# Loads that wait for the third-last store instead of the second-last, in a decode-step gradient kernel

## The chip, the cores and the metric

The kernel runs on one core of a Trainium2 chip. The metric is device time in microseconds (us) of one execution; lower is better. Executions of one kernel agree within about 0.3%.

## The reference, cut to what matters

One decode step of attention over a cache plus a gated MLP, in parallel, and the gradients of all inputs:

```python
xn  = layernorm(x)                                     # x: (1, 1, 640)
q   = xn @ wq                                          # 32 heads of 128
p   = softmax(q @ k_cache^T * 128**-0.5)               # k_cache, v_cache: (1, 32, 8192, 128), bf16
out = x + (p @ v_cache) @ wo + (silu(xn @ w1) * (xn @ w3)) @ w2
# returned: out, and its gradients for x, k_cache, v_cache, wq, wo, w1, w3, w2
```

The caches are 64 tiles of 2 MB (32 heads, K and V). Each is read once, and the gradient for it, a dense tile of the same size, is written once. Together with the weights, their gradients and the instruction fetch, 304.63 MB pass through the DMA engines.

## The kernel before: the parts that matter

A K or V tile fills one of ten SBUF slots. VectorE writes the gradient over the tile in place, the slot is stored, and a later tile is loaded into it. All cache loads and stores go through one function, `fifo`, which issues on the SyncE queue in program order. An issue that has to wait for a semaphore holds up all issues behind it.

```python
def fifo(out_, in_):
    nc.sync.dma_start(out_, in_)

free_slots = [...]                      # ten tiles, 128 x 8192 bf16
pending = [K of head 0, V of head 0, K of head 1, ...]
lag = [1]

def load_next():
    if not pending or len(free_slots) < lag[0]:
        return
    kind, h = pending.pop(0)
    t = free_slots.pop(0)               # the slot that was freed first
    fifo(t[:], (kc if kind == "K" else vc)[h])
    kv_tiles[(kind, h)] = t
...                                     # six loads; four slots lent to the MLP's weights
lag[0] = 2

def store(kind, h):
    t = kv_tiles.pop((kind, h))
    ...
    fifo((dkc if kind == "K" else dvc)[h], t[:])
    free_slots.append(t)
    load_next()
```

With `lag` 2, the load after a store takes not the slot just stored but the one stored before it, and so waits for the landing of the second-last store.

Between heads 1 and 2 the kernel does the MLP. It overwrites the weights in the four lent slots with their gradients, stores these through another queue (POOL's), and gives the slots back, one load each:

```python
nc.gpsimd.dma_start(out_8[...], w2a);  ...;  free_slots.append(mD);  load_next()
for wi in range(2):
    ...
    nc.gpsimd.dma_start(dv[:, 0:NA, :], wa)
    free_slots.append((mA, mB)[wi])
    load_next()
    ...
free_slots.append(mC)
load_next()
```

Of the kernel before, what the change touches and what calls it, by code (L numbers as in the profile page):

```python
# [21 lines left out]
def kernel(  # L22
# [93 lines left out]
    lag = [1]  # L116
# [35 lines left out]
    for _ in range(2):  # L152
        load_next()

    lag[0] = 2

    ident_f = consts.tile([P, P], F32, name="ident_f")
    make_identity(nc, ident_f[:])
# [595 lines left out]
```

## Time and profile before

| | before |
|---|---|
| time, median of the first 3 runs | 751.14 us (750.63 to 751.73) |
| span of the profile | 749.7 us |
| PE / VectorE busy | 79% / 60% |
| DMA, the main data queue alone | 89.1% of 16 engines' span |
| 2 MB store, issue to landing | 22.2 us |
| 2 MB load, issue to landing | 16.6 us (K), 16.7 us (V) |

First the page of before: its busy line (engine, us, share, instructions), its queue table (packets, MB, share of 16 engines' span) and its issue table (count, KB each, median us to landing).

```profile
PE 593.0 (79%) x11263; PEld 565.3 (75%) x11263; DVE 447.7 (60%) x739; ACT 333.3 (44%) x668; POOL 30.4 (4%) x45
...
q1 hardware_dynamic: 22736, 276.39, 89.1%
q0 software_dynamic: 5984, 26.30, 8.7%
q8 instruction: 88, 1.44, 0.7%
...
out_dram<-kv SPq DMA_DIRECT2D x64, 2048.0 KB, 22.2
kv<-in_A_k_cache_dram SPq DMA_DIRECT2D x32, 2048.0 KB, 16.6
```

The three queues add up to 98.5% of all that 16 DMA engines have. No compute engine comes near that.

Where is DMA not full? This is the view by stretches of before. The last two numbers of a line are the DMA share and GB/s.

```profile
120.00:140.00 20.00, 18.25 (x372) 17.54 (x372) 11.65 (x16) 10.59 (x21) 0.00 (x0) 1.00 0.84 319
300.00:660.00 360.00, 298.14 (x5622) 286.91 (x5618) 212.96 (x325) 169.16 (x338) 11.43 (x14) 0.92 1.01 414
730.00:746.00 16.00, 0.00 (x0) 0.00 (x0) 0.00 (x0) 0.00 (x0) 0.00 (x0) 0.50 0.68 286
```

There is one hole, at 120-140 us. The timeline of the SyncE queue in before (start, us taken to issue, what) shows what the queue did there:

```profile
116.70 0.33 SPq L101 DMA_DIRECT2D kv<-in_A_v_cache_dram  x1
130.49 0.33 SPq L101 DMA_DIRECT2D kv<-in_A_k_cache_dram  x1
130.87 1.19 SPq L101 DMA_DIRECT2D out_dram<-kv  x1
```

Between 116.70 and 130.49 us nothing is issued. The load at 130.49 (K of head 6) goes into a slot that held the MLP's w3; its gradient's store on POOL's queue was issued at 90.25 and landed at 130.4. Right behind that load stands the store of head 2's V. VectorE had finished that tile by 111.8 us, as its timeline in before shows (the two halves of V's gradient, then the first half of K's):

```profile
107.36 4.48 DVE L379 TENSOR_TENSOR kv<-qd,P 128x4096 bf16<-128x4096 bf16 x2
111.76 2.28 DVE L379 TENSOR_TENSOR kv<-qd,U 128x4096 bf16<-128x4096 bf16 x1
```

The last thing to read is who among the DMA engines is late. A 2 MB transfer raises its semaphore 16 times as its parts land, and the trace has the time of every increment. One load of before in the steady state (issued 509.89), in us, sorted:

```
before: 517.8 517.9 518.0 518.0 518.1 518.1 518.7 519.8 519.9 520.3 520.5 520.7 520.8 522.6 523.3 526.8
```

Fifteen increments come within 5.5 us and the last one 3.5 us after the fifteenth. One part of every transfer is late; I call whatever carries it the lagging engine. A transfer counts as landed only at the sixteenth increment. Over the transfers issued at 300-660 us, first and last increment lie 8.5 us apart on average (the skew).

### The profile page before, as it was taken

The numbers are of one execution on the slowest core, as the hardware profiler recorded it, in microseconds if no ns is written. First come the engines' busy times: TensorE is split into PE (matmuls) and PEld (weight loads), VectorE is DVE, ScalarE is ACT, GpSimd is POOL, SyncE is SP. The second block draws the span as 40 slices with busy tenths as digits, with TensorE's granted clock in tenths as the row PEclk, the third lists the DMA queues.
The fourth block names the chain that finished last, engine by engine and source line by source line (L and its number), as shares of the span: only waits on it lengthen the run. The fifth ranks groups of instructions, "written<-read, shape, count | busy, mean of one in ns | idle before, by whom it ended". The sixth has DMA issues, their size and how long they took to land.

```text
span 749.7 us, 25013 instructions
## 1 busy us (share of the span) xinstructions
PE 593.0 (79%) x11263; PEld 565.3 (75%) x11263; DVE 447.7 (60%) x739; ACT 333.3 (44%) x668; POOL 30.4 (4%) x45
## 2 busy tenths in 40 slices
PE   1987798999999868798786978879688898878810
PEld 1885598988998868698686868878688887868800
DVE  4269837677667645657464664657367475646670
ACT  1641065555565435445354544435355354535400
POOL 0100200000000100000000000000000000000000
PEclk9997799999999999999898998989899799999955
DMA  8999998999999999999999999999999999999995
GB/s 329 389 413 420 418 418 353 378 425 426 416 424 430 424 421 413 423 410 420 417 392 416 415 425 397 424 412 420 422 392 414 418 421 404 413 408 415 426 428 224
DMA packets 29136, 304.63 MB, mean 406 GB/s; under 512 B 2836, under 2 KB 5972, under 8 KB 12644
## 3 DMA queue, kind: packets, MB, share of 16 engines
q1 hardware_dynamic: 22736, 276.39, 89.1%
q0 software_dynamic: 5984, 26.30, 8.7%
q8 instruction: 88, 1.44, 0.7%
q10 hardware_dynamic: 308, 0.33, 0.2%
q14 instruction: 20, 0.16, 0.1%
HBM read 151.67 MB, written 151.34 MB: 404 GB/s over the span
## 4 chain that ended last, share of the span: by engine, by line
DMA 59%; PE 27%; DVE 8%; issue 2%; ACT 1%; SPq 1%; ACTq 0%; DVEq 0%
DMA out_dram<-kv 39%; DMA kv<-in_A_k_cache_dram 15%; PE pT L274 11%; DMA kv<-in_A_v_cache_dram 4%; PE hb L358 4%; DVE kv L379 3%; PE dA L293 3%; PE sA L293 3%; PE hb L373 3%; DVE U L365 1%; PE dh_ps L462 1%; PE acc L536 1%; PE gu_ps L451 1%; PE sA L320 1%; DVE kv L539 0%
## 5 line engine op out<-in xcount | busy, mean ns | idle before, releaser
L274 PE MATMUL pT<-ident_f,kv 128*128 128x128 f32 x2048 | 335.2, 288 | 67.8 <-DMA kv<-in_A_k_cache_dram 60.1
L276 ACT COPY KT<-pT 128x512 f32<-128x512 f32 x512 | 299.3, 586 | 183.8 <-PE pT L274 151.1
L274 PEld LDWEIGHTS pT<-ident_f,kv 128*128 128x128 f32 x2048 | 223.5, 145 | 72.2 <-issue 68.7
L293 PEld LDWEIGHTS <-KT 128*128 128x128 bf16 x4096 | 196.0, 100 | 19.9 <-issue 12.8
L379 DVE TENSOR_TENSOR kv<-qd,U 128x4096 bf16<-128x4096 bf16 x64 | 146.0, 2284 | 0.0
L379 DVE TENSOR_TENSOR kv<-qd,P 128x4096 bf16<-128x4096 bf16 x64 | 143.4, 2282 | 0.0
L293 PE MATMUL dA<-cz,KT 128*128 128x64 bf16 x2048 | 106.6, 196 | 8.8 <-ACT qd L310 6.6
L293 PE MATMUL sA<-cz,KT 128*128 128x64 bf16 x2048 | 103.0, 192 | 1.4 <-issue 1.4
L358 PEld LDWEIGHTS <-kv 128*128 128x128 bf16 x2048 | 80.8, 105 | 16.5 <-issue 16.5
L358 PE MATMUL hb<-P,kv 128*128 128x64 bf16 x2048 | 81.6, 201 | 14.3 <-DVE U L365 14.3
L375 ACT COPY od_g<-hb 128x2 f32<-128x2 f32 x32 | 5.1, 160 | 159.1 <-PE hb L373 159.1
L373 PE MATMUL hb<-U,kv 128*128 128x64 bf16 x2048 | 70.4, 194 | 5.0 <-issue 4.9
L373 PEld LDWEIGHTS <-kv 128*128 128x128 bf16 x2048 | 66.7, 98 | 5.7 <-issue 5.7
L349 DVE SCALAR_TENSOR_TENSOR U<-dA,P 128x64 bf16<-128x64 f32 x32 | 7.4, 233 | 90.2 <-PE dA L293 90.2
L316 DVE TENSOR_REDUCE mrow<-sA 128x1 f32<-128x64 f32 x32 | 7.2, 224 | 83.4 <-PE sA L293 83.4
L365 DVE SCALAR_TENSOR_TENSOR U<-dA,hb,P 128x128 bf16<-128x128 f32 x32 | 11.4, 355 | 35.3 <-PE hb L363 35.3
L429 DVE SCALAR_TENSOR_TENSOR wq_g<-wq_g,side 128x512 bf16<-128x512 bf16 x40 | 27.3, 682 | 0.0
L340 DVE RECIPROCAL rZ<-sA 128x1 f32<-128x1 f32 x32 | 5.4, 168 | 35.9 <-PE sA L334 35.0
L233 DVE SCALAR_TENSOR_TENSOR side<-wo_g,g_bc 128x640 bf16<-128x640 bf16 x32 | 26.2, 817 | 0.3
L323 DVE TENSOR_REDUCE negM<-sA 128x1 f32<-128x128 f32 x32 | 9.3, 291 | 18.6 <-PE sA L320 18.6
L424 POOL DMA_DIRECT2D out_dram<-wo_g x8 | 6.1, 761 | 291.1 <-DVE cz L298 255.7
L433 POOL DMA_DIRECT2D out_dram<-wq_g x8 | 6.9, 863 | 256.9 <-DVE wq_g L431 256.9
(134 smaller groups left out, 310.2 us busy)
## 6 DMA issues: line engine op xcount, KB each, us to landing
out_dram<-kv SPq DMA_DIRECT2D x64, 2048.0 KB, 22.2
kv<-in_A_k_cache_dram SPq DMA_DIRECT2D x32, 2048.0 KB, 16.6
kv<-in_A_v_cache_dram SPq DMA_DIRECT2D x32, 2048.0 KB, 16.7
out_dram<-wo_g POOLq DMA_DIRECT2D x8, 640.0 KB, 12.6
out_dram<-wq_g POOLq DMA_DIRECT2D x8, 640.0 KB, 13.5
wq_g<-in_A_wq_dram POOLq DMA_DIRECT2D x7, 640.0 KB, 13.9
wo_g<-in_A_wo_dram POOLq DMA_DIRECT2D x7, 640.0 KB, 19.6
kv<-in_B_w_dram SPq DMA_DIRECT2D x2, 1728.0 KB, 16.5
```

Source lines behind the costliest of these rows:

```text
L233: nc.vector.scalar_tensor_tensor(junk[:], G_["wo"][:, hh, :], 1.0, g_bc[:], ALU.mult, ALU.mult, accum_out=G_["do"][:, hh:hh + 1])
L274: nc.tensor.transpose(pT[:, k * P:(k + 1) * P], W3[:, 4 * c + k, :], ident_f[:])
L276: nc.scalar.copy(KT[:].rearrange("p k w -> p (k w)"), pT[:])
L293: nc.tensor.matmul(S_[kind][:, 0:J], lhsT=KTb[:, k, par, :], rhs=S_["cz"][:, o:o + J], start=(i == 0 and par == 0), stop=(par == 1), skip_ ...
L320: nc.tensor.matmul(S_["K"][:, J:J + P], lhsT=S_["mrow"][:].to_broadcast([P, P]), rhs=ident_f[:], start=False, stop=True, skip_group_check= ...
L323: nc.vector.tensor_reduce(S_["negM"][:], S_["K"][:, J:J + P], AX.X, ALU.max, negate=True)
L358: nc.tensor.matmul(S_["hb"][:, 0:RW], lhsT=V3[:, j, :], rhs=S_["P2"][:, j, 0:1].to_broadcast([P, RW]), start=(j == 0), stop=(j == J - 1), ...
L365: nc.vector.scalar_tensor_tensor(S_["U2"][:], S_["V"][:, 0:J].unsqueeze(2).to_broadcast([P, J, 2]), S_["hb"][:, 2 * RW:2 * RW + 1], S_["P2 ...
L373: nc.tensor.matmul(S_["hb"][:, RW:2 * RW], lhsT=K3[:, j, :], rhs=S_["U2"][:, j, 0:1].to_broadcast([P, RW]), start=False, stop=(j == J - 1) ...
L379: nc.vector.tensor_tensor(dst[:, lo * DH:hi * DH].rearrange("p (j a b) -> p j a b", a=DH // 2, b=2), vec.rearrange("p (a b) -> p a b", b=2 ...
L429: nc.vector.scalar_tensor_tensor(wq_g[:, ci, :], wq_g[:, ci, :], 1.0, dqb, ALU.mult, ALU.mult, accum_out=dxa[:, ci, g:g + 1])
L451: nc.tensor.matmul(gu_ps[0:rows, wi, b:b + 1], lhsT=wrow(wi, ci)[:, b * P:b * P + rows], rhs=xn_col_bf[:, ci:ci + 1], start=(ci == 0), sto ...
```

## The change

The intent is to let SyncE issue stores earlier and wait less. The diff is one number:

```diff
-    lag[0] = 2
+    lag[0] = 3
```

Load k still reuses the k-th freed slot, and still needs that slot's store to have landed. What changes is the order in the queue: from the third store on, each store goes ahead of one load. Around the hole (a number is a head):

```
before: ... load V5, load K6, store V2, load V6, store K2, load K7 ...
after:  ... load V5, store V2, load K6, store K2, load V6, store V3, load K7 ...
```

## The prediction

> **What bounds the kernel.** The DMA engines, not compute. The page of before: 304.63 MB in a span of 749.7 us; its queue table sums to over 98% of 16 engines' span, against PE 79% and DVE 60%. In 10 us windows the DMA share is about 1.0 except at 0-10 us (0.74), 120-140 us (0.81 and 0.87, at 340 and 298 GB/s instead of about 420) and the last 10 us. PE's waits for K loads (60.1 us, 21 waits) follow from the full queue: a load lands 16.6 us after its issue.
>
> The semaphore landings in the trace (16 increments per transfer) say more. First and last increment of a 2 MB transfer lie 8 to 10 us apart in the steady state: some engines lag. The leading engines complete transfers 4.9 us apart, then pause for the next issue; the last increments are 4.9 to 6.4 us apart without a pause. The laggard's work sets the time; SyncE's wait on stores (581.6 us) is back-pressure. The Trainium skill's "DMA: Bandwidth & Descriptors", section "Why a DMA increments its semaphore by 16 and not by 1", says that the engines of a transfer finish independently; this trace agrees.
>
> **What the change does.** It adds and removes no transfer. Load k reuses the k-th freed slot and needs that store's landing in both kernels. In the queue's order each store from the third on moves ahead of one load: load k stands behind store k+2 instead of k+1. At a load's issue about 5 transfers are in flight instead of 3. Loads come about one transfer (5 us) later in the stream. In the steady state about 4 finished tiles wait to be stored (near 433 us head 16's V is stored while PE is in head 19), so the stores that go first are ready and DMA stays full either way. I expect no gain there: the laggard's bytes are the same.
>
> **Where it can gain.** SyncE sits from 117 to 130.5 us on a load whose slot is freed by a POOL-queue weight-gradient store (issued 90.25, landed 130.4), while the store of V2, computed by about 112 us, is stuck behind it (issued 130.87). The queue drains: over 120-140 us 10 x (80 + 122) us GB/s is missing, about 4.8 us of transfer, 3.2 us of it idle. In the new order V2's store goes first, near 117 us: 5 us of work. I count 2 to 4 us, all on the critical path since DMA is full from there on; the total drops by about 2.5 us.
>
> **Where it can lose.** Deeper queues let the leading engines run further ahead (skew 12-18 us); if their traffic slows the laggard (stores 5.3-5.6 us ungated in the tail, 5.2-5.35 gated), 1 to 3 us come back. The last load lands about 5 us later, but in before it landed at 699.6, the last store was issued at 717.3 and the laggard was busy to 748.6: over 20 us of slack.
>
> **Prediction.** 748.6 us, 80% range 745 to 752. Over 2% faster 0.02, within 2% 0.96, over 2% slower 0.02.
>
> **What would show it.** V2's store issued near 117 us; no dip at 120-140 us; store latency up from 22.2 to near 32 us, load latency from 16.6 to 22-26; landing skew above 10 us; PE waits for loads up, not down; busy times and bytes unchanged.
>
> **What would make it wrong.** That the finished-tile backlog is too short, so that loads are held for stores still being computed and DMA gaps appear every head (slower by 1% or more); or that read/write order or depth itself changes the rate of the DMA engines.

## The result, and the profile after

| | before | after |
|---|---|---|
| time, median | 751.24 us (4 runs) | 747.95 us (4 runs, 747.36 to 749.01) |
| span of the profile | 749.7 us | 745.6 us |
| 2 MB store / K load, issue to landing | 22.2 / 16.6 us | 31.8 / 26.9 us |
| mean skew, issued at 300-660 us | 8.5 us | 17.9 us |

The ratio is 0.9958 with a 95% interval of 0.9941 to 0.9975: a real gain of about 0.4%, within 2%. The output is correct.

The page after, same rows as before:

```profile
PE 596.1 (80%) x11263; PEld 568.4 (76%) x11263; DVE 447.8 (60%) x739; ACT 333.4 (45%) x668; POOL 30.4 (4%) x45
...
q1 hardware_dynamic: 22736, 276.39, 88.5%
q0 software_dynamic: 5984, 26.30, 8.8%
q8 instruction: 88, 1.44, 0.7%
...
out_dram<-kv SPq DMA_DIRECT2D x64, 2048.0 KB, 31.8
kv<-in_A_k_cache_dram SPq DMA_DIRECT2D x32, 2048.0 KB, 26.9
```

The work is the same. Every transfer of a K or V tile takes about 10 us longer to land, because two more transfers stand in the queue before it.

The SyncE timeline after, in the same place:

```profile
116.55 0.33 SPq L101 DMA_DIRECT2D kv<-in_A_v_cache_dram  x1
116.93 0.81 SPq L101 DMA_DIRECT2D out_dram<-kv  x1
130.25 0.33 SPq L101 DMA_DIRECT2D kv<-in_A_k_cache_dram  x1
```

The load of K6 goes out at the same time as before, but the store of V2 no longer waits for it: 116.93 instead of 130.87 us. At 145.65 us head 2's K store has also fully landed, where before head 2's V store had only just landed (145.53). The run is then exactly one 2 MB store ahead.

The stretches after:

```profile
120.00:140.00 20.00, 17.91 (x375) 17.14 (x373) 11.53 (x18) 10.86 (x23) 0.00 (x0) 1.00 1.00 402
300.00:660.00 360.00, 296.64 (x5631) 285.92 (x5629) 213.81 (x324) 168.54 (x337) 11.44 (x14) 0.94 1.01 422
730.00:746.00 16.00, 0.00 (x0) 0.00 (x0) 0.00 (x0) 0.00 (x0) 0.00 (x0) 0.50 0.06 27
```

The hole is filled in this execution. In the profiles of the three repeats below it is filled in part: 363, 381 and 382 GB/s at 120-140 us, against 319 in before. There is also a second difference, and it invites a wrong story. In the long middle the mean rate rose from 414 to 422 GB/s, as if the deeper queue made DMA faster. The third line shows where that goes: in the last 16 us the DMA share is 0.06, which is one engine of sixteen (1/16 = 0.0625) at work. The landing increments of the last store say the same:

```
before: 739.2 739.3 739.3 739.4 739.5 739.9 740.1 740.5 742.0 742.0 742.1 742.8 743.1 743.3 743.7 748.6
after:  724.8 724.9 724.9 725.0 725.0 725.0 726.3 726.3 727.5 727.6 727.7 728.1 728.4 728.9 729.5 744.5
```

After the change, fifteen parts are done by 729.5 us and one works alone until 744.5. The fifteen finished 14 us earlier than in before; the sixteenth, which sets the time, 4.1 us earlier.

### The profile page after: what moved, and what is told of

The parts are those of the page before. It is cut to its first block, busy times and chain, and to the rows that moved or that the text cites. A ratio compares the mean times of both kernels' runs of the same rounds, so it can differ in the third digit from the quotient of the medians.

```text
span 745.6 us, 25013 instructions
## 1 busy us (share of the span) xinstructions
PE 596.1 (80%) x11263; PEld 568.4 (76%) x11263; DVE 447.8 (60%) x739; ACT 333.4 (45%) x668; POOL 30.4 (4%) x45
## 3 DMA queue, kind: packets, MB, share of 16 engines
q8 instruction: 88, 1.44, 0.7%
## 4 chain that ended last, share of the span: by engine, by line
DMA 48%; PE 39%; DVE 8%; issue 2%; ACT 1%; SPq 0%; ACTq 0%; DVEq 0%
DMA kv<-in_A_k_cache_dram 31%; PE pT L274 17%; DMA out_dram<-kv 13%; PE hb L358 6%; PE hb L373 4%; PE sA L293 4%; DMA kv<-in_A_v_cache_dram 4%; PE dA L293 4%; DVE kv L379 3%; DVE U L365 1%; PE sA L320 1%; PE dh_ps L462 1%; PE hb L363 1%; PE acc L536 1%; PE gu_ps L451 1%
## 5 line engine op out<-in xcount | busy, mean ns | idle before, releaser
L274 PE MATMUL pT<-ident_f,kv 128*128 128x128 f32 x2048 | 337.1, 289 | 67.4 <-DMA kv<-in_A_k_cache_dram 62.4
## 6 DMA issues: line engine op xcount, KB each, us to landing
out_dram<-kv SPq DMA_DIRECT2D x64, 2048.0 KB, 31.8
kv<-in_A_k_cache_dram SPq DMA_DIRECT2D x32, 2048.0 KB, 26.9
kv<-in_A_v_cache_dram SPq DMA_DIRECT2D x32, 2048.0 KB, 26.9
```

Of the source, the lines that this page charges most:

```text
L274: nc.tensor.transpose(pT[:, k * P:(k + 1) * P], W3[:, 4 * c + k, :], ident_f[:])
```

## The experiments

Two theories for the gain. **Theory A**: the single early stall. The store of V2 stuck behind the load of K6 left the lagging engine without work; filling that hole is the whole gain. **Theory B**: depth. With five transfers in flight instead of three, DMA runs at 422 instead of 414 GB/s in the steady state.

A question behind both: **why is one engine late?** The theory is that it also carries the PE's instruction fetch (queue q8); the rival is that the fetch is spread over all engines and costs nothing. (The runs below were made to decide this and do not; the kept traces speak against the theory.)

Twelve runs in three batches, each batch with the changed kernel itself and with its own runs of before (medians 751.82, 751.83 and 751.66 us). All were correct except one that is wrong on purpose.

| run | median us | ratio to before | 95% interval |
|---|---|---|---|
| changed kernel, batch 1 / 2 / 3 | 747.84 / 748.71 / 749.03 | 0.9948 / 0.9959 / 0.9956 | 0.9937-0.9960 / 0.9946-0.9972 / 0.9943-0.9970 |
| one exchange only, batch 1 / 3 | 749.32 / 748.54 | 0.9968 / 0.9951 | 0.9955-0.9981 / 0.9937-0.9965 |
| deep later only, batch 1 | 751.80 | 0.9997 | 0.9984-1.0011 |
| deep early only, batch 3 | 748.15 | 0.9953 | 0.9938-0.9968 |
| fourth-last store, batch 1 | 748.37 | 0.9953 | 0.9941-0.9965 |
| more small PE pairs, batch 2 | 752.40 | 1.0010 | 0.9997-1.0024 |
| the same columns in wide pairs, batch 2 | 749.72 | 0.9974 | 0.9961-0.9987 |
| fewer PE pairs, batch 2 | 742.83 | 0.9881 | 0.9866-0.9896 |
| half the pairs, right result, batch 3 | 806.17 | 1.0717 | 1.0696-1.0737 |

The changed kernel as the yardstick of its batch:

> The changed kernel again, in the rounds of the next three: about 748 us, 0.996 of before.

> The changed kernel, in the rounds of the next three: about 748 us.

> The changed kernel, in the rounds of the next three: about 748 us, ratio 0.995 to 0.996.

It came out as expected three times, at 0.9948 to 0.9959.

### One exchange only

The kernel before, but the load due when `mC` comes back is put off until after the next store. The queue differs from before's in one place: store V2 goes ahead of load K6. All later loads wait for the second-last store.

```diff
+    owed = []
 ...
         free_slots.append(mC)
-        load_next()
+        owed.append(1)
 ...                                    # in store()
         free_slots.append(t)
         load_next()
+        if owed:
+            owed.pop()
+            load_next()
```

> The kernel before with one single exchange in the SyncE queue: the store of head 2's V goes ahead of the load of head 6's K; everything later waits for the second-last store as before. Theory (the gain is one early stall of the lagging DMA engine): the whole gain, 747 to 749 us, ratio 0.995 to 0.997; V2's store issued near 117 us, no dip at 120-140 us, while the landing skew stays at 8 to 11 us and the rate over 300-660 us stays at before's 413 GB/s. Rival (a deeper queue in the steady state, 424 instead of 413 GB/s, is the gain): 750.5 to 752 us, ratio 0.999 to 1.001.

Measured 749.32 us, 0.9968. V2's store went out at 119.55 us, the skew stayed at 8.4 us and the steady rate at 414 GB/s, as in before. In this view by stretches of the one-exchange kernel only the first line has changed against before:

```profile
120.00:140.00 20.00, 18.46 (x377) 17.75 (x375) 11.84 (x16) 10.84 (x22) 0.00 (x0) 1.00 0.98 397
300.00:660.00 360.00, 298.25 (x5602) 287.31 (x5599) 211.68 (x329) 171.38 (x344) 11.46 (x14) 0.93 1.01 414
```

So most of the gain needs no depth at all. But beside the changed kernel of its batch (0.9948) 0.2% seemed to be missing, with intervals that just overlap. It was run again:

> The single exchange again, beside the changed kernel: if all of the gain is the one stall, the two agree within 0.5 us; if the other early exchanges count too, it lies 1 to 2 us above (0.997 against 0.995), as in the first batch.

The second time it was 748.54 us (0.9951), beside 749.03 us (0.9956) for the changed kernel. The gap of the first batch did not repeat. Within what these runs resolve, the single exchange gives the whole gain.

### Deep later only

```diff
+        if kind == "V" and h == 4:
+            lag[0] = 3
         load_next()
```

> The kernel before up to the store of head 4's V, then the third-last store as in the changed kernel. Theory: no gain, 750 to 752 us, ratio 0.9985 to 1.001, although the rate over 300-660 us rises to about 424 GB/s and the skew to 18-20 us; the dip at 120-140 us is there as in before. Rival (deeper queue): the whole gain, 747 to 749 us, ratio 0.995 to 0.997.

Measured 751.80 us, 0.9997: nothing. Yet everything that theory B points to is there; this is the view by stretches of this run:

```profile
120.00:140.00 20.00, 18.64 (x379) 17.91 (x379) 12.03 (x16) 11.17 (x22) 0.00 (x0) 1.00 0.88 333
300.00:660.00 360.00, 295.93 (x5630) 285.26 (x5630) 213.02 (x326) 167.00 (x335) 12.19 (x15) 0.93 1.01 421
730.00:746.00 16.00, 0.93 (x3) 0.58 (x3) 2.57 (x15) 0.00 (x0) 0.86 (x1) 0.50 0.29 112
```

The rate is 421 GB/s and the skew 17.9 us, as in the changed kernel, the hole at 120-140 us is still there, and the time is before's. Theory B has fallen. A higher mean rate over sixteen engines says nothing about the one that ends last.

### Deep early only

The complement: third-last store until V of head 4 is stored, then one owed load and second-last from there on.

```diff
+        if kind == "V" and h == 4:
+            lag[0] = 2
+            load_next()
```

> The complement of the run that is deep only later: third-last store until the store of head 4's V, then one owed load, then second-last. Theory (only the early stage counts): as the changed kernel within 0.5 us, ratio 0.995 to 0.996, with skew 8 to 11 us. Rival (the rest of the gain comes from depth later on): as the single exchange, 0.997.

Measured 748.15 us, 0.9953, with a skew of 8.2 us. The gain is made in the early stage, and it is kept without depth.

### The fourth-last store

```diff
-    lag[0] = 3
+    lag[0] = 4
```

> The fourth-last store instead of the third-last. Theory: nothing more to gain, 747 to 749 us, ratio 0.995 to 0.997; skew up to about 20 to 30 us, store latency near 42 us; the lagging engine's own work unchanged. Rival (depth is worth 3 us a step): 744 to 745.5 us, ratio 0.991 to 0.9925. Third possibility (stores not ready, loads held): slower than the changed kernel, 750 us or more.

Measured 748.37 us, 0.9953: the same as the changed kernel. A store now takes 39.0 us to land and the mean skew is 22 us. One more step of depth buys nothing, and it costs nothing either. Stores that are not ready yet do hold the queue now: SyncE waits 183.1 us in total for tiles that VectorE is still writing, against 31.9 us in the changed kernel and 7.4 us in before. DMA stays full all the same, with a share of 1.01 at 300-660 us.

### Why one engine is late: more and fewer PE instructions

PE's 11263 weight loads and 11263 matmuls are 22526 instructions, and q8 moved 1.44 MB: 64 bytes each, in 88 packets of 16 KB. The Trainium skill says in "Runtime: NRT & Kernel Launch", section "Instruction fetch mechanics", that a sequencer refills its instruction memory in 16 KiB blocks of 256 instructions through a DMA queue of its own, and calls the cost mostly hidden. The size agrees with this trace. Whether the cost is hidden was tried on the changed kernel.

```diff
+        for _ in range(64):             # after dq_sum(h); into a part added to the PSUM tile
+            nc.tensor.matmul(hb[:, 256:256 + RW], lhsT=ident_bf[:], rhs=ident_bf[:, 0:RW], start=False, ...)
```

> The changed kernel with 64 more small weight-load and matmul pairs per head (64 columns each, into an unused part of a PSUM tile; result unchanged). 2048 pairs are 4096 instructions; at before's 1.44 MB for 22526 PE instructions that is 262 KB, 16 more packets of the instruction queue. Theory (one DMA engine ends last because it also carries the PE's instruction fetch): each packet costs that engine 0.3 to 0.6 us (a 16 KB packet takes 0.611 us when alone), so 5 to 10 us more, 752.5 to 758 us. Rival (the fetch is spread evenly over 16 engines): at most 0.6 us more, 748 to 749 us. If PE time itself counts: this run and the wide one rise alike.

The control has the same columns in a quarter of the instructions:

```diff
+        for _ in range(16):
+            nc.tensor.matmul(hb[:, 256:512], lhsT=ident_bf[:], rhs=<ident_bf twice>, start=False, ...)
```

> The changed kernel with the same 4096 extra columns per head in 16 wide pairs of 256 columns: about the same extra PE streaming time, a quarter of the instructions (4 packets of fetch). Theory (fetch on one engine): 1 to 2.5 us more, 749 to 750.5 us. Rival (PE time counts): as much as the run with 64 small pairs. Rival (nothing counts): 748 us.

And the other direction, with a wrong dq:

```diff
-        for j in range(J):
+        for j in range(J - 1, J):       # dq_sum: 1 of 64 pairs left
```

> The changed kernel with 1 instead of 64 pairs in the dq sum of each head; wrong result on purpose (the gradients that come from dq). 2016 pairs fewer are 258 KB of fetch, 15.75 packets. Theory (fetch on one engine): 5 to 9.5 us less, 738 to 743 us. Rival (spread fetch, nothing gained): 747 to 748.5 us.

Against the changed kernel of the batch (748.71 us): 16 packets more cost 3.7 us, 4 more cost 1.0 us, and 16 fewer gained 5.9 us, that is 0.23, 0.25 and 0.37 us a packet. The first is below the 5 us expected, and the first two are not clean. From the pages and the waits of the three runs (small pairs, wide pairs, fewer pairs; the waits give us in total, times, longest):

```profile
PE 634.1 (84%) x13311; PEld 602.6 (80%) x13311; DVE 447.7 (60%) x739; ACT 332.2 (44%) x668; POOL 30.4 (4%) x45
...
q8 instruction: 104, 1.70, 0.9%
...
PE pT L274 <- DMA kv<-in_A_k_cache_dram: 5.4, 1, 5.4
```

```profile
PE 635.1 (85%) x11775; PEld 601.2 (80%) x11775; DVE 448.0 (60%) x739; ACT 333.0 (45%) x668; POOL 30.4 (4%) x45
...
q8 instruction: 92, 1.51, 0.8%
...
PE pT L274 <- DMA kv<-in_A_k_cache_dram: 26.0, 12, 5.3
```

```profile
PE 554.9 (75%) x9247; PEld 526.1 (71%) x9247; DVE 446.8 (60%) x739; ACT 334.2 (45%) x668; POOL 30.4 (4%) x45
...
q8 instruction: 72, 1.18, 0.6%
...
PE pT L274 <- DMA kv<-in_A_k_cache_dram: 77.0, 25, 5.0
```

With the 64 small pairs PE hardly waits for K any more (5.4 us, against 62.9 us in the changed kernel of this batch), so PE itself may be the limit there, and that run proves little. The wide pairs are half way to it: the waits are down to 26.0 us, and PE makes up 50% of the chain of work that ended last, against 28% in the changed kernel. The run with fewer pairs has no such flaw: PE waits longer for K loads than in the changed kernel (77.0 us), so PE is not its limit, and the time is 5.9 us shorter. The last store's last increment moved too, from 746.1 us in the changed kernel of the batch to 739.6 us. If 16 packets (0.26 MB) were spread over 16 engines, each would be relieved of one packet, 0.6 us by the 0.611 us that a 16 KB packet took in the tail where one engine worked alone. Ten times that was measured.

It is tempting to conclude that most of the fetch rides on the late engine. The kept traces speak against it. They give the start and length of every DMA packet, though not its engine. In the tail of the changed kernel, where only the late engine works, a 4 KB packet of POOL's queue starts at 735.61 us, a 16 KB packet of the data queue at 735.76, the next two at 736.38 and 736.53: packets of two queues take turns, and each adds its own time. So a fetch packet on the late engine should put some 0.6 us between two of its landings (an estimate from the 0.611 us). The time from one sixteenth increment to the next is the late engine's own work for one transfer. The table gives it for the four traces of the changed kernel at 272-716 us, where the sixteenth increment is always at least 2.0 us behind the fifteenth. The packets are counted in windows set 0.49 us earlier, which is the time from a last packet to its increment; transfers that a fetch packet touches only in part are left out.

| late engine's time for one transfer | cases | mean us | range us |
|---|---|---|---|
| load, no fetch packet anywhere in that time | 4 | 4.86 | 4.85-4.89 |
| load, a whole fetch packet in that time | 58 | 4.86 | 4.80-4.90 |
| load, POOL packets in that time | 55 | 5.91 | 4.71-6.53 |
| store, no fetch packet anywhere in that time | 20 | 5.21 | 5.16-5.37 |
| store, a whole fetch packet in that time | 31 | 5.39 | 5.26-5.72 |

POOL packets are in no line but the third. POOL's packets lengthen a load; a fetch packet does not lengthen it at all, and the difference in the stores is 0.2 us. So the fetch packets in these loads ran on other engines (inferred, since no packet names its engine), and most of those in the stores cannot have been on the late one either. What the table does show is that the late engine's stores take longer than its loads, 5.2 to 5.4 against 4.86 us, while its last store, with the other engines done, took 4.84 us. At about 0.45 us for each of 64 stores that is 29 us (an estimate). Why one engine's stores are slow stays open.

Nor did the gain of the run with fewer pairs come packet by packet. By the landing of the 18th K or V store (282.3 to 283.9 us in the four traces of the changed kernel) its one trace was already at 280.3 us, 2.0 to 3.6 us of a final lead of 4.9 to 6.6 us, with 4 or 5 of the 16 packets saved by 280 us. The runs with more pairs were further ahead there (277.7 us with small, 279.2 with wide pairs) and lost it later. Fewer pairs also mean less PE work and other times for all that waits for it, and no run separates these from the fetch. So the 5.9 us are real, their cause is not shown, and 0.37 us is no price of a packet.

### Half the pairs with the right result

The run with fewer pairs was faster, so the next attempt was to compute the sums, rightly, with fewer PE instructions. In the o and dq sums, the changed kernel uses the cache rows as weights, 64 pairs each. This version uses the probabilities as weights and two rows of the cache tile as 256 moving columns, 32 pairs each, plus small products and copies to gather the result into a column.

```diff
-        for j in range(lo, hi):
-            nc.tensor.matmul(hb[:, 0:RW], lhsT=V3[:, j, :], rhs=P2[:, j, 0:1].to_broadcast([P, RW]), ...)
+        for j in range(lo, hi, 2):
+            nc.tensor.matmul(hb[0:2, 256:512], lhsT=P2[:, j:j + 2, 0], rhs=V[:, j * DH:(j + 2) * DH], ...)
```

> The changed kernel with the sums o and dq computed the other way round: probabilities as weights (2 columns), two 128-wide rows of V or K as 256 moving columns, 32 pairs instead of 64 for each sum, and 4 small products and 3 copies per head to gather the result; right result. About 54 pairs per head fewer, some 13 packets of instruction fetch; at the 0.25 to 0.37 us a packet that the earlier runs show: 3.5 to 5 us less than the changed kernel, 743 to 745 us, ratio 0.989 to 0.991. If the longer matmuls make PE the limit, it is slower than the changed kernel.

A miss: 806.17 us. The result is right and q8 is down to 74 packets, but PE is now the limit. The chain of waits of this run, and the two groups that took the place of the sums (us busy and mean ns after the first bar):

```profile
PE 79%; DVE 11%; DMA 4%; ACT 3%; issue 2%; ACTq 0%; SPq 0%; DVEq 0%
...
L360 PE MATMUL hb<-kv,P 128*2 128x256 bf16 x1024 | 122.1, 272 | 14.3 <-DVE U L367 14.3
L377 PE MATMUL hb<-kv,U 128*2 128x256 bf16 x1024 | 116.9, 272 | 15.8 <-ACT KT L374 15.8
```

The two sums keep PE busy for 239 us, against 152 us in before (81.6 and 70.4), and the small gathering products add another 33.5 us. The kernel before had no such slack to give: it kept PE busy for 593 of 750 us. No version with a right result beats the changed kernel clearly; the single exchange and the early-only version equal it.

## Why the prediction was right

It said 748.6 us in a range of 745 to 752, within 2%. Measured: 747.95 us. Point by point:

- **DMA bounds the kernel, and in it one late engine.** Right, and plainer than foretold: in the tail after the change one engine works alone for 13 us (731.3 to 744.2). Why that engine is late is not shown.
- **No gain from depth in the steady state.** Right. The deep-later run shows it: ratio 0.9997 with all signs of depth present.
- **The gain is the stall at 117-130.5 us.** Right. V2's store went out at 116.93 us where "near 117" was said, and the one-exchange run has the whole gain within what the runs resolve.
- **Size.** About 2.5 us was said, 3.3 us by the medians and 4.1 us by the spans was measured. The term that was too pessimistic is "1 to 3 us come back" because the leading engines' traffic slows the laggard. The deep-later run, where that could have cost most, lost nothing (751.80 against 751.82 us). Of the 5 us of one store by which the changed run leads at 145.65 us, 4.1 us are left at the end of its profile.
- **Latencies and skew.** Stores "near 32 us": 31.8. Loads "22-26": 26.9, since two transfers more stand ahead of a load, not one. Skew "12-18": 17.9 on average, 21 at most.
- **"PE waits for loads up."** Wrong, and without effect on the time. PE's waits for K and V loads were 60.1 + 7.1 = 67.2 us and became 62.4 + 4.6 = 67.0. A later landing did not add to them. That these waits follow the pace of the lagging engine, which did not change, and not the latency of a load is my reading; no run isolates it.
- **Tail slack.** Right: the last load landed at 700.4 us, the last store was issued at 718.1, and the late engine was busy until 744.5.

## What to carry to other kernels

In a queue that issues in order, look for the one wait that holds up work which is ready, and move that work ahead of it; here a single exchange of two transfers was worth as much as a deeper queue throughout. When DMA is full, ask which engine ends last before believing a mean rate: the increments of one transfer's semaphore show it, and a mean that rises while the last increment stays is no gain. When a run gains, look in its trace where the gain arises before dividing it by a count: here the number of instruction packets fitted the late engine's delay, and the landings of single transfers did not. Before cutting PE instructions, check that the replacement leaves PE below its limit.

## What the Trainium skill lacked or had wrong

- "Runtime: NRT & Kernel Launch", section "Instruction fetch mechanics", calls the cost of a 16 KiB block mostly hidden. Nothing here shows otherwise: the late engine's loads took 4.86 us with and without a fetch packet in that time, and the 5.9 us of the run with fewer pairs stay unexplained. The page does not say on which DMA engines the fetch runs.
- "DMA: Bandwidth & Descriptors", section "Latency and other measured facts", says that engines 7 and 15 are usually the slower ones. Here one engine lags, and it seems to be another (an exception to "usually", not a contradiction): the two last outputs have five rows each, and after the change four of the first one's five parts landed at about 730.1 us and the fifth at 733.6 us (730.6 and 734.5 us for the second one), so the late engine is among the five that they use. By the same page, section "Why a DMA increments its semaphore by 16 and not by 1", those are the lowest-numbered five. No run here shows an engine's number.
- No page has a DMA engine whose stores are slower than its loads (5.2 to 5.4 against 4.86 us for the late engine here).
- No page has the skew between a transfer's first and sixteenth increment (8.5 us at three transfers in flight, 17.9 at five, 22 with the fourth-last store), and that the mean DMA rate can rise (414 to 421 GB/s in the deep-later run) with no effect on the time.
